# Keys and queries by token loads and DMA transposes, two output banks and a reordered start in a windowed-attention and softplus-MLP kernel

## The chip, the cores and the metric

One core of one Trainium2 chip. The metric is device microseconds of one execution of the whole kernel; the figure compared is the median of repeated runs. The engines are TensorE (PE; its weight loads are PEld), VectorE (DVE), ScalarE (ACT), GpSimd (POOL) and SyncE (SP), which here only issues DMAs.

## What is computed

Eight batches of eight heads, 576 positions, 64 elements per head. A query sees the keys within 32 positions; eight positions (global_idx) see all and are seen by all. The result of attention, 4,608 tokens by 512, goes through two matrix products with a softplus between.

```
scores = scale * np.matmul(q, k.transpose(0, 1, 3, 2))
mask = np.abs(pos[:, None] - pos[None, :]) <= 32
mask = mask | is_global[:, None] | is_global[None, :]
attn = softmax(where(mask, scores, -1e9))
x = np.matmul(attn, v)            # then (B, S, H*D) as 4608 x 512
h = x @ w_in                      # 512 -> 2048
g = np.maximum(h, 0.0) + np.log1p(np.exp(-np.abs(h)))
out = g @ w_out                   # 2048 -> 512
```

## The kernel before

**Attention of a batch.** A batch is four pairs of heads (p). Keys and queries are needed with the head's elements on the partitions (KT, QT: 128 partitions = two heads of 64, five blocks of 120 or 96 positions, each block followed by eight columns for the global positions). `load_runs` (L100) brings a batch of k to SBUF in one DMA on SP (float32, six positions to a partition, pieces of 1536 bytes) and a batch of q in one DMA on POOL's queue that casts to bfloat16. `cast_runs` (L137) reorders them on POOL into kqb, two heads at a time. `transposes` (L287) turns one pair: six PE transposes of 96 columns into one PSUM bank (tp, one bank in the main part) and, through `spread_columns` (L322), two DVE copies into KT or QT (L325, L327) and one or two small POOL copies (L330 to L333) that put in the global columns. For batches 3 to 7 these come from glob_T, which `global_columns` (L466) makes with PE from rows that `gather_rows` (L130) fetched, sixteen DMAs on POOL's queue. For batch 2 they come from `columns_of_2` (L458).

`products` (L343) multiplies keys and queries, `exponentials` (L358) is ACT's Exp, `mask` (L372) is DVE's product. `over_keys` (L385) forms both the sums (values all one) and the weighted values, in PSUM (av). `inv_ln` and `inv_exp` (L413, L421) make the reciprocal on ACT as exp(-ln), `scale_x` (L430) multiplies on DVE into xT. `glob_norm` (L446, DVE) and `glob_out` (L452, eight POOL copies, L455) put the rows of the global positions into xT. The values of a batch come in five DMAs of up to 120 tokens (`load_v`, L109, pieces of 256 bytes, on SP), are cast by POOL (`cast_v`, L143), and batch 2's are loaded by six casting DMAs on POOL's queue (`load_v_cast`, L118).

**The two products.** Nine tiles of 512 tokens. `mm1(n, kf)` (L478) makes one of 16 blocks of 128 columns of h: four matmuls into a bank h (two of them), then Exp and Ln with bias 1 on ACT, 512 columns each, into gts[n]. `mm2(n, s)` (L491) does a quarter of the products of 128 rows of the output: four matmuls into the one bank o; after the fourth quarter DVE copies to ot (two buffers) and SP stores.

**What sets the order.** The instruction order on every engine is written by hand. Ahead of the tile loop stand batch 0 and the begin of batch 1. Then (L683):

```
    for n in range(n_tiles + 1):
        for s in range(16):
            if n < n_tiles:
                mm1(n, s)
            attend(16 * n + s, 0)
            if n:
                mm2(n - 1, s)
            attend(16 * n + s, 1)
```

`attend` issues what the plan holds for that slot (16n+s) and half. `at(slot, half, f, ...)` fills the plan (L517), in the order of the calls. STARTS (L522) gives for each pair, in half slots, where its attention begins: batch 2 at slot 16, batch 3 at 28, batch 4 at 41, then every 16 slots. Loads stand some 20 slots ahead, casts some 12. An engine goes through its own instructions in this order and waits for semaphores only, so POOL and SP may run ahead of PE or hold it up. The first_rz buffer (L337, one of the two gt buffers) holds batch 0's reciprocals.

Of the kernel before, what the change touches and what calls it, by code (L numbers as in the profile page):

```python
# [11 lines left out]
FP32 = mybir.dt.float32  # L12
BF16 = mybir.dt.bfloat16
I32 = mybir.dt.int32
ALU = mybir.AluOpType
ACTF = mybir.ActivationFunctionType
# [3 lines left out]
P = 128  # L20
WIN = 32
KW = 120
NG = 8

ST = [120, 120, 120, 120, 96]
NTL = 5
WLO = [max(0, 128 * t - 40) for t in range(NTL)]
WHI = [128 * t + 160 for t in range(4)] + [512 + 96 + NG]
NPOS = WHI[-1]
SPLIT = 288  # L30
RUN = 6
NQ = 96
# [3 lines left out]
GOFF = {0: 0, 1: 160, 4: 360, 2: 0, 3: 200}  # L36
# [4 lines left out]
def kernel(  # L41
# [10 lines left out]
    nc = tc.nc  # L52
    B, H, S, D = q.shape
    NP = H // 2
    HD = H * D
    d_model, d_ff = moe_w_in.shape
    n_tokens = out.shape[0]
    KD, KF, NT = d_model // P, d_ff // P, 512
# [20 lines left out]
    KT = const.tile([P, NP, NTL, P], BF16)  # L79
    QT = const.tile([P, NP, NTL, P], BF16)  # L80
    V1 = [const.tile([P, NTL, HD], BF16, name=f"V1_{i}") for i in range(2)]
    runs = const.tile([NQ, H, RUN * D], FP32, name="k_f")
    v_f = const.tile([P, NTL, HD], FP32)
    GB = B - 3
    glob_2 = {n: const.tile([P, NP, NG], BF16, name=f"{n}_g2") for n in "kq"}
# [23 lines left out]
    def load_v(b, heads=slice(0, H)):  # L109
        for t in range(NTL):  # L110
            nc.sync.dma_start(out=v_f[:ST[t], t].rearrange("p (h d) -> p h d", d=D)[:, heads],
                              in_=v[b, heads, KW * t:KW * t + ST[t], :].rearrange("h s d -> s h d"))

    def load_v_rows(b):
        nc.sync.dma_start(out=v_f[KW:P], in_=v_rows[:, (b - 1) * HD:b * HD].unsqueeze(1).to_broadcast([NG, NTL, HD]))
# [171 lines left out]
    def transposes(n, b, p, copy=nc.vector.tensor_copy, unread=0):  # L287

        parts = [(slice(0, P), lambda r: kqb[n, b][:, r, p * P:(p + 1) * P])]
        if n == "q" and b < 2:  # L290
            parts = [(slice(64 * e, 64 * e + 64), lambda r, e=e: raw[b][:, 2 * p + e, r * D:(r + 1) * D]) for e in range(2)]
        if b == 1 and p:
            if n == "k":
                both[p] = region("tp")
            ps = both[p][:, 0:512] if n == "k" else both.pop(p)[:, 512:1024]
        else:
            ps = bank()[:]
        tb = ps.bitcast(BF16)
        for _ in range(unread):
            nc.tensor.matmul(out=ps, lhsT=junk[:, 0:P], rhs=junk[:], start=True, stop=True)  # L300
        for r in range(RUN):
            for o, of in parts:
                nc.tensor.transpose(out=tb[o, r * NQ:(r + 1) * NQ], in_=of(r), identity=ident_bf[:NQ, :NQ])  # L303
        if b < 2:
            g = ps[:, 384:384 + NG]
            for r in range(RUN):
                for o, of in parts:
                    nc.tensor.matmul(out=g[o], lhsT=of(r), rhs=onehot[:NQ, r, :],
                                     start=(r == 0), stop=(r == RUN - 1), skip_group_check=True)
        else:  # L310
            copy = nc.vector.tensor_copy
            g = glob_2[n][:, p] if b == 2 else glob_T[n][:, p].rearrange("p (g b) -> p b g", b=GB)[:, b - B + GB]
        spread = lambda: spread_columns(n, b, p, tb, g, copy)
        if b == 1 and p:
            both.setdefault((p, "copies"), []).append(spread)
            if n == "q":
                for f in both.pop((p, "copies")):
                    f()
        else:
            spread()  # L320
# [22 lines left out]
    def products(b, p, grp):  # L343
        sc = SC[p, grp] = region("sc")[:].rearrange("p (e c) -> p e c", e=2)
        biased = (b, p) in BIASED
        if biased:
            for e in range(2):
                nc.tensor.matmul(out=sc[:, e, 0:GW[grp]], lhsT=ident_bf[:], rhs=biases[grp], start=True, stop=False,
                                 skip_group_check=True)
        for i, t in enumerate(GRP[grp]):  # L350
            w = WHI[t] - WLO[t]
            for e in range(2):
                r = slice(64 * e, 64 * e + 64)
                nc.tensor.matmul(out=sc[:, e, GOFF[t]:GOFF[t] + w], lhsT=KT[r, p, t, :],  # L354
                                 rhs=QT[r, p].rearrange("p t c -> p (t c)")[:, WLO[t]:WHI[t]],
                                 start=not biased, stop=(not biased or i == len(GRP[grp]) - 1), skip_group_check=biased)

    def exponentials(b, p, grp):  # L358
# [119 lines left out]
    def mm1(n, kf):  # L478
        if kf == 0:
            gts[n] = work.tile([P, KF, NT], BF16, tag="gt", bufs=2, name="gt")  # L480
        hp = psum["pool"].tile([P, NT], FP32, tag="h", bufs=2)
        for kd in range(KD):
            nc.tensor.matmul(out=hp[:], lhsT=w_in_t[:, kd, kf * P:(kf + 1) * P], rhs=xT[:, kd, n * NT:(n + 1) * NT],  # L483
                             start=(kd == 0), stop=(kd == KD - 1))
        e = work.tile([P, NT], FP32, tag="e", bufs=2)
        nc.scalar.activation(out=e[:], in_=hp[:], func=ACTF.Exp)  # L486
        nc.scalar.activation(out=gts[n][:, kf, :], in_=e[:], func=ACTF.Ln, bias=1.0)  # L487

    ops = {}

    def mm2(n, s):  # L491
        i, part = s // 4, s % 4
        if part == 0:
            ops[n] = psum["pool"].tile([P, d_model], FP32, tag="o", name="o")
        op = ops[n]
        for kf in range(4 * part, 4 * part + 4):
            nc.tensor.matmul(out=op[:], lhsT=gts[n][:, kf, i * P:(i + 1) * P], rhs=w_out_t[:, kf, :],  # L497
                             start=(kf == 0), stop=(kf == KF - 1))
        if part == 3:
            ot = work.tile([P, d_model], FP32, tag="ot", bufs=2)  # L500
            nc.vector.tensor_copy(ot[:], op[:])  # L501
            nc.sync.dma_start(out=out[n * NT + i * P:n * NT + (i + 1) * P, :], in_=ot[:])

    CW = 512

# [11 lines left out]
    def at(g, half, f, *a):  # L517
        plan.setdefault((g, half), []).append((f, a))
# [11 lines left out]
    for p in range(NP):  # L530
        for n in "kq":
            at(8 + p // 2, 0, cast_runs, n, 2, pair_heads(p), nc.gpsimd.tensor_copy)
    at(9, 0, load_v_cast, 2)
    for i, n in enumerate("kq"):
        at(14 + i, 0, columns_of_2, n)
        at(27, i, global_columns, n)
        for g in range(NG):
            at(18 + g, 0, gather_rows, n, g)
    LOADS, CASTS = {3: (18, 20, 19)}, {3: (23, 26)}
    for b in range(1, B):  # L540
        g0 = 16 * (b - 1)
        if b > 2:
            loads = LOADS.get(b, (g0 - 22, g0 - 20, g0 - 17))
            at(loads[0], 1, load_runs, "k", b, every)
            at(loads[1], 1, load_runs, "q", b, every)
            at(loads[2], 1, load_v, b)
            at(loads[2], 1, load_v_rows, b)
            casts = CASTS.get(b, (g0 - 12, g0 - 9))
            for p in range(NP):
                for i, n in enumerate("kq"):  # L550
                    at(casts[0] + (4 * i + p) // 3, 0, cast_runs, n, b, pair_heads(p), nc.gpsimd.tensor_copy)
            for t in range(NTL):
                at(casts[1] + t // 3, 0, cast_v, b, t, nc.gpsimd)
        steps = {}

        def step(h, f, *a):
            steps.setdefault(h, []).append((f, a))

        for p in range(NP):
            if b == 1:  # L560

                to_transposes, to_scores, to_sums = (2 if p == 1 else 4 * p + 2), 4 * p + 4, 4 * p + 6
                to_inverse = to_x = to_sums
            else:
                h, pair = STARTS[4 * b - 8 + p], STARTS[4 * b - 7 + p] - STARTS[4 * b - 8 + p]
                to_transposes, to_scores, to_sums = h, h + pair // 2 + (pair == 7), h + pair
                to_inverse, to_x = to_sums + 1, to_sums + 2
            if (b, p) != (1, 0):
                step(to_transposes, transposes, "k", b, p)
                step(to_transposes + (b > 1), transposes, "q", b, p)  # L570
                for grp in range(2):
                    step(to_scores, scores, b, p, grp)
                for grp in range(2):
                    if (b, p) not in BIASED:
                        step(to_scores, mask, p, grp)
            step(to_sums, sums, b, p)
            step(to_sums, values, b, p)
            step(to_sums, inv_ln, b, p)
            step(to_inverse, glob_sums, b, p, 0)
            step(to_inverse, inv_exp, p)  # L580
            step(to_x, scale_x, b, p)
        step(to_x + (b > 1), glob_norm, b)
        step(to_x + (b > 1), glob_out, b)
        for h in sorted(steps):
            for f, a in sorted(steps[h], key=lambda fa: fa[0] is not transposes):
                at(h // 2, h % 2, f, *a)
# [138 lines left out]
```

## Time and profile before

| what | value |
|---|---|
| median of 14 runs | 368.59 us (365.36 to 371.0) |
| profiled execution | 368.92 us |
| its span | 367.3 us, mean clock granted to PE 0.995 |
| PE busy | 346.3 us, 94% |
| ACT busy | 272.8 us, 74% |
| DVE busy | 169.0 us, 46% |
| POOL busy | 132.1 us, 36% |
| SP's issues of token loads of v | 40, median 0.936 us each, landing after 5.2 us (median) |

The page gives busy times, the span in 40 slices, the chain of work that ended last and the costliest groups. In a timeline a row is: start, duration, engine, line, operation, written tile <- read tiles, shape, count, and in brackets the idle time before it and what ended it. Matmuls are pipelined, so durations on PE overlap: what a group takes is read from start to start. The profiled execution lies 1.6 us over its span, and this is the sum's base; the median of the runs is 0.3 us lower.

### The profile page before, as it was taken

Reading aid. Unit: us, or ns where it says so; the run is one execution under the profiler, and the core shown is the slowest. Engines: PE = TensorE matmul, PEld = TensorE weight load, DVE = VectorE, ACT = ScalarE, POOL = GpSimd, SP = SyncE. Lnnn points to the kernel's source line nnn. Section 1 sums busy time; section 2 is a strip of 40 time slices with the busy share of each in tenths; the row PEclk is TensorE's granted clock in tenths of the full one; section 3 lists DMA queues with packets and bytes.
Section 4 is the critical chain, followed back from the end, with each engine's and each line's share of the span. In section 5 each row is a group of like instructions: output and inputs, shape, how many; then the busy total and the mean of one; then the engine's idle time right before and its main releaser. Section 6 shows DMA issues by size and latency. Waiting matters only on the chain.

```text
span 367.3 us, 7712 instructions
## 1 busy us (share of the span) xinstructions
PE 346.3 (94%) x2981; PEld 173.5 (47%) x2981; DVE 169.0 (46%) x476; ACT 272.8 (74%) x433; POOL 132.1 (36%) x301
## 2 busy tenths in 40 slices
PE   7898897999899999999999999999999999999984
PEld 3565453454455545554555455545554444444431
DVE  7863432275576555655555556555553001001011
ACT  3677997687788888888888888888888667776500
POOL 7953949795157206430733074302001000000000
PEclk9999999899999999999999999999999999999999
DMA  7999999996628065806590758100000100100111
GB/s 174 199 225 216 216 195 231 90 211 149 98 59 142 14 160 93 168 32 157 95 168 29 159 94 166 32 29 31 29 32 34 52 29 30 57 29 30 57 57 57
DMA packets 63108, 37.87 MB, mean 103 GB/s; under 512 B 41672, under 2 KB 58224, under 8 KB 63072
## 3 DMA queue, kind: packets, MB, share of 16 engines
q1 hardware_dynamic: 44768, 27.63, 31.7%
q0 software_dynamic: 18160, 9.75, 20.2%
q8 instruction: 23, 0.38, 0.4%
q14 instruction: 13, 0.11, 0.1%
q10 hardware_dynamic: 144, 0.01, 0.0%
HBM read 37.56 MB, written 9.55 MB: 128 GB/s over the span
## 4 chain that ended last, share of the span: by engine, by line
PE 72%; POOL 7%; DMA 7%; DVE 5%; ACT 4%; issue 3%; POOLq 0%; DVEq 0%; ACTq 0%
PE o L497 33%; PE hp L483 28%; PE av L396 5%; PE tp L303 3%; PE sc L354 3%; DMA k_f<-in_k_dram 3%; DMA v_f<-in_v_dram 2%; DMA q_raw<-in_q_dram 2%; DVE ot L501 2%; POOL V L122 1%; POOL V L145 1%; DVE KT L325 1%; ACT rz L418 1%; ACT ex L365 1%; POOL kb L140 1%
## 5 line engine op out<-in xcount | busy, mean ns | idle before, releaser
L483 PE MATMUL hp<-xT,w_in_t 128*128 128x512 bf16 x576 | 148.6, 381 | 3.2 <-POOL xT L455 2.7
L497 PE MATMUL o<-w_out_t,gt 128*128 128x512 bf16 x576 | 146.5, 380 | 4.5 <-DVE ot L501 4.5
L486 ACT ACTIVATE e<-hp 128x512 f32<-128x512 f32 x144 | 85.9, 597 | 49.0 <-PE hp L483 46.9
L487 ACT ACTIVATE gt<-e 128x512 bf16<-128x512 f32 x144 | 90.7, 630 | 4.7
L497 PEld LDWEIGHTS <-gt 128*128 128x128 bf16 x576 | 54.5, 98 | 69.1 <-issue 9.9
L483 PEld LDWEIGHTS <-w_in_t 128*128 128x128 bf16 x576 | 52.3, 98 | 65.4 <-issue 7.7
L501 DVE COPY ot<-o 128x512 f32<-128x512 f32 x36 | 24.9, 691 | 73.2 <-PE o L497 71.5
L455 POOL COPY xT<-xg 128x4 bf16 x64 | 16.4, 256 | 95.9 <-DVE xg L450 92.5
L365 ACT ACTIVATE ex<-sc 128x1008 bf16<-128x1008 f32 (+1 forms) x56 | 48.5, 918 | 0.4 <-PE sc L354 0.4
L374 DVE TENSOR_TENSOR ex<-ex,mask 128x1008 bf16<-128x1008 bf16 (+1 forms) x48 | 34.1, 718 | 25.1 <-ACT ex L365 24.3
L325 DVE COPY KT<-tp 128x480 bf16<-128x480 bf16 x31 | 20.3, 655 | 35.4 <-PE tp L303 24.9
L145 POOL CAST V<-v_f 128x512 bf16<-128x512 f32 (+3 forms) x45 | 22.1, 531 | 27.5 <-DMA v_f<-v_global_rows 22.1
L140 POOL CAST kb<-k_f 96x768 bf16<-96x768 f32 x30 | 25.1, 856 | 4.2 <-DMA k_f<-in_k_dram 4.2
L406 DVE TENSOR_REDUCE gs<-av 128x8 f32<-128x32 f32 x64 | 12.0, 187 | 30.2 <-ACT rz L418 26.7
L418 ACT ACTIVATE rz<-av 128x616 f32<-128x616 f32 x28 | 19.0, 680 | 7.2 <-PE av L396 6.6
L325 DVE COPY QT<-tp 128x480 bf16<-128x480 bf16 x29 | 19.0, 657 | 10.5 <-PE tp L303 9.8
L434 DVE TENSOR_TENSOR xT<-av,rz 128x480 bf16<-128x480 f32 x28 | 18.4, 657 | 11.4 <-ACT rz L422 11.3
L140 POOL COPY qb<-q_raw 96x768 bf16<-96x768 bf16 x24 | 19.2, 825 | 10.7 <-DMA q_raw<-in_q_dram 8.8
L354 PE MATMUL sc<-QT,KT 64*128 64x200 bf16 (+2 forms) x320 | 20.2, 241 | 2.3 <-DVE xT L436 1.6
L422 ACT ACTIVATE rz<-rz 128x616 f32<-128x616 f32 x28 | 19.7, 703 | 0.2
L354 PEld LDWEIGHTS <-KT 64*128 64x128 bf16 x320 | 10.6, 94 | 18.6 <-issue 13.9
L396 PE MATMUL av<-ex,V 128*64 128x160 bf16 (+1 forms) x336 | 16.1, 229 | 1.3 <-POOL V L145 1.3
(126 smaller groups left out, 267.5 us busy)
## 6 DMA issues: line engine op xcount, KB each, us to landing
out_dram<-ot SPq DMA_DIRECT2D x36, 256.0 KB, 2.0
v_f<-in_v_dram SPq DMA_DIRECT2D x24, 240.0 KB, 5.7
k_f<-in_k_dram SPq DMA_DIRECT2D x5, 1152.0 KB, 10.7
k_f<-in_k_dram SPq DMA_DIRECT2D x12, 288.0 KB, 7.6
q_raw<-in_q_dram POOLq DMA_DIRECT2D x6, 576.0 KB, 6.0
w_in_t<-in_moe_w_in_dram POOLq DMA_DIRECT2D x4, 512.0 KB, 7.4
w_out_t<-in_moe_w_out_dram POOLq DMA_DIRECT2D x4, 512.0 KB, 13.9
v_f<-in_v_dram SPq DMA_DIRECT2D x6, 192.0 KB, 5.2
```

The lines of the kernel that those rows point to most:

```text
L140: copy(kqb[n, b][:, :, D * heads.start:D * heads.stop].rearrange("p r (h d) -> p h r d", d=D), (runs if n == "k" else raw[b])[:, heads].re ...
L145: eng.tensor_copy(V1[b % 2][:rows, t, cols], v_f[:rows, t, cols])
L325: copy(dst[:, p, 0:4, 0:KW].rearrange("p t (q r) -> p t q r", r=RUN), spread[:, 0:4 * NQT].rearrange("p (t q) r -> p t q r", q=NQT))
L354: nc.tensor.matmul(out=sc[:, e, GOFF[t]:GOFF[t] + w], lhsT=KT[r, p, t, :], rhs=QT[r, p].rearrange("p t c -> p (t c)")[:, WLO[t]:WHI[t]], s ...
L365: nc.scalar.activation(out=ex, in_=sc[:, :, 0:GW[grp]], func=ACTF.Exp, scale=SCALE)
L374: nc.vector.tensor_tensor(out=ex, in0=ex, in1=masks[grp][:, 0:GW[grp]].unsqueeze(1).to_broadcast([P, 2, GW[grp]]), op=ALU.mult)
L396: nc.tensor.matmul(out=av[64 * e:64 * e + 64, OFF + lo:OFF + hi], lhsT=weight(t, e), rhs=exps[p, grp][rows, e, c:c + hi - lo], start=(firs ...
L483: nc.tensor.matmul(out=hp[:], lhsT=w_in_t[:, kd, kf * P:(kf + 1) * P], rhs=xT[:, kd, n * NT:(n + 1) * NT], start=(kd == 0), stop=(kd == KD ...
L486: nc.scalar.activation(out=e[:], in_=hp[:], func=ACTF.Exp)
L487: nc.scalar.activation(out=gts[n][:, kf, :], in_=e[:], func=ACTF.Ln, bias=1.0)
L497: nc.tensor.matmul(out=op[:], lhsT=gts[n][:, kf, i * P:(i + 1) * P], rhs=w_out_t[:, kf, :], start=(kf == 0), stop=(kf == KF - 1))
L501: nc.vector.tensor_copy(ot[:], op[:])
```

## The change

1. *Output banks.* In tiles 1 to 7 the odd row groups write their products into the bank tp, the even ones stay in o. In the last tile all four use the two banks h. The last row group is made in two halves of 256 columns, each with 16 matmuls, a copy and a store.
2. *Tile 0's logarithm.* The exponentials of tile 0 go into first_rz (four areas of 512), and one Ln of 1024 columns serves two blocks.
3. *Batch 2's values* (`load_v_cast(2)`) move from slot 9 to slot 12.
4. *Tokens.* For batches 3 to 7, k, q and v come by token, five DMAs each on SP, spread over slots; k and q share one float32 buffer (kq_f, the former `runs`). POOL casts each to a bfloat16 tile with the tokens on the partitions, SP issues one DMA transpose for all pairs of a batch (128 x 2560 bfloat16, SBUF to SBUF) into KT/QT (even batches) or new tiles (odd ones), and POOL copies in the global columns of all pairs at once. The PE transposes of these batches and their DVE copies go. For batches 3 and 4 POOL first clears partitions 96 to 128 of the token tiles.

```
+    kq_f = const.tile([P, H * RUN * D], FP32, name="kq_f")
+    runs = kq_f[:NQ].rearrange("p (h c) -> p h c", h=H)
...
+    def tokens(n, b):
+        if (n, b) not in tok:
+            fresh = b < 5
+            tok[n, b] = work.tile([P, NP * NTL * P], BF16, tag=f"{n}b", bufs=2, name=f"{n}t") if fresh else tok[n, b - 2]
+            if fresh:
+                nc.gpsimd.memset(tok[n, b][96:P], 0.0)
+        return tok[n, b][:].rearrange("p (a t c) -> p a t c", a=NP, t=NTL)
+    def load_tokens(n, b, t):
+        o = kq_f if n != "v" else v_f[:].rearrange("p t c -> p (t c)")
+        nc.sync.dma_start(out=o[:ST[t], t * HD:(t + 1) * HD].rearrange("p (h d) -> p h d", d=D),
+                          in_=src[n][b, :, KW * t:KW * t + ST[t], :].rearrange("h s d -> s h d"))
+    def cast_tokens(n, b, t):
+        nc.gpsimd.tensor_copy(tokens(n, b)[:ST[t], :, t, :],
+                              kq_f[:ST[t], t * HD:(t + 1) * HD].rearrange("p (a c) -> p a c", a=NP))
+    def turn(n, b):
+        if b % 2:
+            turned[n, b] = work.tile([P, NP, NTL, P], BF16, tag="raw", bufs=2, name=f"{n}T")
+        else:
+            turned[n, b] = KT if n == "k" else QT
+        nc.sync.dma_start_transpose(out=turned[n, b][:].rearrange("p a t c -> p (a t) c"), in_=tok[n, b][:])
+    def spread_globals(n, b):
+        dst = turned[n, b]
+        g = glob_T[n][:].rearrange("p a (g b) -> p a b g", b=GB)[:, :, b - B + GB].unsqueeze(2)
+        if n == "k":
+            nc.gpsimd.tensor_copy(dst[:, :, :, KW:P], g.to_broadcast([P, NP, NTL, NG]))
+        else:
+            nc.gpsimd.tensor_copy(dst[:, :, 0:4, KW:P], g.to_broadcast([P, NP, 4, NG]))
+            nc.gpsimd.tensor_copy(dst[:, :, 4:5, ST[4]:ST[4] + NG], g)
...
+        if n == 0:
+            c = NT * (kf % 4)
+            e = first_rz[:].bitcast(FP32)
+            nc.scalar.activation(out=e[:, c:c + NT], in_=hp[:], func=ACTF.Exp)
+            if kf % 2:
+                nc.scalar.activation(out=gts[n][:, kf - 1:kf + 1, :].rearrange("p k c -> p (k c)"),
+                                     in_=e[:, c - NT:c + NT], func=ACTF.Ln, bias=1.0)
+            return
...
-            ops[n] = psum["pool"].tile([P, d_model], FP32, tag="o", name="o")
+            last = n == n_tiles - 1
+            ops[n] = psum["pool"].tile([P, d_model], FP32, tag="h" if last else "tp" if n and i % 2 else "o",
+                                       bufs=2 if last else 1, name="o")
...
+        if n == n_tiles - 1 and i == NT // P - 1:
+            if part % 2 == 0:
+                cols = slice(0, 256) if part == 0 else slice(256, 512)
+                if part:
+                    op = psum["pool"].tile([P, d_model], FP32, tag="h", bufs=2, name="o")
+                products_out(n, i, op[:, cols], range(KF), cols)
+                store(n, i, op[:, cols], cols)
+            return
...
-    at(9, 0, load_v_cast, 2)
+    at(12, 0, load_v_cast, 2)
...
+    def loads(b):
+        s0 = STARTS[4 * b - 8] // 2
+        if b == 3:
+            k0, kt, q0, qt, v0 = s0 - 12, s0 - 7, s0 - 8, s0 - 3, s0 - 5
+        elif b == 4:
+            k0, kt, q0, qt, v0 = s0 - 15, s0 - 10, s0 - 11, s0 - 6, s0 - 8
+        else:
+            k0, kt, q0, qt, v0 = s0 - 23, s0 - 15, s0 - 16, s0 - 8, s0 - 9
+        for n, first, last in (("k", k0, kt), ("q", q0, qt), ("v", v0, None)):
+            for t in range(NTL):
+                slot = first + (t // 2 if b < 5 else t)
+                at(slot, t % 2 if b < 5 else 1, load_tokens, n, b, t)
+                if n == "v":
+                    at(slot + 2, 1, cast_v, b, t, nc.gpsimd)
+                else:
+                    at(slot + 2, 0, cast_tokens, n, b, t)
+            if n == "v":
+                at(first, 0, load_v_rows, b)
+            else:
+                at(last, 0, turn, n, b)
+                at(max(last + 2, 28), 0, spread_globals, n, b)
...
-                step(to_transposes, transposes, "k", b, p)
-                step(to_transposes + (b > 1), transposes, "q", b, p)
+                if b < 3:
+                    step(to_transposes, transposes, "k", b, p)
+                    step(to_transposes + (b > 1), transposes, "q", b, p)
```

More of the change, by code (lines that the diff above doesn't have):

```diff
@@ L81 @@
     V1 = [const.tile([P, NTL, HD], BF16, name=f"V1_{i}") for i in range(2)]
-    runs = const.tile([NQ, H, RUN * D], FP32, name="k_f")
+    kq_f = const.tile([P, H * RUN * D], FP32, name="kq_f")
+    runs = kq_f[:NQ].rearrange("p (h c) -> p h c", h=H)
     v_f = const.tile([P, NTL, HD], FP32)
@@ L112, in load_v @@
                               in_=v[b, heads, KW * t:KW * t + ST[t], :].rearrange("h s d -> s h d"))
+    tok, turned = {}, {}
+    def tokens(n, b):
[26 more added lines that the diff above has]
+            nc.gpsimd.tensor_copy(dst[:, :, 4:5, ST[4]:ST[4] + NG], g)
     def load_v_rows(b):
@@ L311, in transposes @@
             copy = nc.vector.tensor_copy
-            g = glob_2[n][:, p] if b == 2 else glob_T[n][:, p].rearrange("p (g b) -> p b g", b=GB)[:, b - B + GB]
+            g = glob_2[n][:, p]
         spread = lambda: spread_columns(n, b, p, tb, g, copy)
@@ L349, in products @@
                                  skip_group_check=True)
+        kT, qT = turned.get(("k", b), KT), turned.get(("q", b), QT)
         for i, t in enumerate(GRP[grp]):
@@ L353, in products @@
                 r = slice(64 * e, 64 * e + 64)
-                nc.tensor.matmul(out=sc[:, e, GOFF[t]:GOFF[t] + w], lhsT=KT[r, p, t, :],
-                                 rhs=QT[r, p].rearrange("p t c -> p (t c)")[:, WLO[t]:WHI[t]],
+                nc.tensor.matmul(out=sc[:, e, GOFF[t]:GOFF[t] + w], lhsT=kT[r, p, t, :],
+                                 rhs=qT[r, p].rearrange("p t c -> p (t c)")[:, WLO[t]:WHI[t]],
                                  start=not biased, stop=(not biased or i == len(GRP[grp]) - 1), skip_group_check=biased)
@@ L489, with products_out, store @@
     ops = {}
+    def products_out(n, i, op, blocks, cols=slice(0, 512)):
+        for kf in blocks:
+            nc.tensor.matmul(out=op, lhsT=gts[n][:, kf, i * P:(i + 1) * P], rhs=w_out_t[:, kf, cols],
+                             start=(kf == 0), stop=(kf == KF - 1))
+    def store(n, i, op, cols=slice(0, 512)):
+        ot = work.tile([P, d_model], FP32, tag="ot", bufs=2)
+        nc.vector.tensor_copy(ot[:, cols], op)
+        nc.sync.dma_start(out=out[n * NT + i * P:n * NT + (i + 1) * P, cols], in_=ot[:, cols])
     def mm2(n, s):
@@ L493, in mm2 @@
         if part == 0:
-            ops[n] = psum["pool"].tile([P, d_model], FP32, tag="o", name="o")
+            last = n == n_tiles - 1
+            ops[n] = psum["pool"].tile([P, d_model], FP32, tag="h" if last else "tp" if n and i % 2 else "o",
+                                       bufs=2 if last else 1, name="o")
         op = ops[n]
-        for kf in range(4 * part, 4 * part + 4):
-            nc.tensor.matmul(out=op[:], lhsT=gts[n][:, kf, i * P:(i + 1) * P], rhs=w_out_t[:, kf, :],
-                             start=(kf == 0), stop=(kf == KF - 1))
+        if n == n_tiles - 1 and i == NT // P - 1:
[6 more added lines that the diff above has]
+            return
+        products_out(n, i, op[:], range(4 * part, 4 * part + 4))
         if part == 3:
-            ot = work.tile([P, d_model], FP32, tag="ot", bufs=2)
-            nc.vector.tensor_copy(ot[:], op[:])
-            nc.sync.dma_start(out=out[n * NT + i * P:n * NT + (i + 1) * P, :], in_=ot[:])
+            store(n, i, op[:])
     CW = 512
@@ L538 @@
             at(18 + g, 0, gather_rows, n, g)
-    LOADS, CASTS = {3: (18, 20, 19)}, {3: (23, 26)}
+    def loads(b):
[19 more added lines that the diff above has]
+                at(max(last + 2, 28), 0, spread_globals, n, b)
     for b in range(1, B):
@@ L542 @@
         if b > 2:
[L543 to L553, printed above, removed]
+            loads(b)
         steps = {}
```

## The prediction

> **What bounds the kernel now.** I read the page's shares first, then the busy time by stage, then each stage's PE timeline.
>
> ```profile
> PE 346.3 (94%) x2981; PEld 173.5 (47%) x2981; DVE 169.0 (46%) x476; ACT 272.8 (74%) x433; POOL 132.1 (36%) x301
> PE 72%; POOL 7%; DMA 7%; DVE 5%; ACT 4%; issue 3%; POOLq 0%; DVEq 0%; ACTq 0%
> ...
> 127.00:163.50 36.50, 36.07 (x312) 18.43 (x310) 21.25 (x55) 30.49 (x48) 15.07 (x34) 1.00 0.54 114
> ...
> 281.00:345.70 64.70, 64.18 (x295) 28.63 (x294) 7.42 (x13) 45.38 (x76) 1.62 (x8) 1.00 0.10 37
> 345.70:367.30 21.60, 14.59 (x65) 6.13 (x63) 3.46 (x5) 0.57 (x1) 0.00 (x0) 0.99 0.16 61
> ```
>
> The last three rows (columns: PE, PEld, DVE, ACT, POOL, granted clock, DMA share, GB/s) are one batch of the steady part, the tiles after attention and the tail. In the steady part PE is busy 36.07 of 36.5 us, and ACT, the next, 30.49. Time there is PE's stream. The tail is not: 14.59 of 21.6.
>
> The PE timeline of one pair of heads in the steady part (start, duration):
>
> ```profile
> 140.76 0.42 PE L303 MATMUL tp<-ident_bf,kb 96*128 96x96 bf16 x6
> 141.11 0.58 PE L396 MATMUL av<-ex,ones 128*64 128x160 bf16 x12
> ...
> 142.02 1.04 PE L483 MATMUL hp<-xT,w_in_t 128*128 128x512 bf16 x4
> 142.89 0.42 PE L303 MATMUL tp<-ident_bf,qb 96*128 96x96 bf16 x6
> 143.15 1.03 PE L497 MATMUL o<-w_out_t,gt 128*128 128x512 bf16 x4
> ```
>
> Start to start, the key transposes take 0.35 us and the query ones 0.26. The tail, and the one stall at the head of tile 1:
>
> ```profile
> 351.01 3.61 PE L497 MATMUL o<-w_out_t,gt 128*128 128x512 bf16 x16 [0.78 <-DVE ot L501]
> ...
> 354.67 0.69 DVE L501 COPY ot<-o 128x512 f32<-128x512 f32 x1 [3.70 <-PE o L497]
> ...
> 355.41 3.61 PE L497 MATMUL o<-w_out_t,gt 128*128 128x512 bf16 x16 [0.78 <-DVE ot L501]
> ...
> 57.04 4.45 POOL L122 DMA_DIRECT2D V<-in_v_dram  x5
> 61.49 2.06 POOL L455 COPY xT<-xg 128x4 bf16 x8
> ...
> 63.60 1.87 PE L483 MATMUL hp<-xT,w_in_t 128*128 128x512 bf16 x4 [2.04 <-POOL xT L455]
> ```
>
> Each tail group waits for the copy that frees the one bank o. At 63.60 PE waits for eight POOL copies that stood behind five DMA issues.
>
> **Part 1, banks and tail.** Groups start every 4.40 us (351.01, 355.41). Sixteen 512-column matmuls at the steady 0.216 (0.864 for four) take 3.46. With two banks the 0.94 between vanishes, also ahead of the first (346.62 instead of 345.69): 4 x 0.94 = 3.8 us. The last rows in halves are 32 matmuls of 256 columns, the same columns; a weight load with its transpose of 96 columns runs at 0.26/6 = 0.044 us, so 0.108 per matmul covers the loads. After the last matmul the copy has 256 columns: from the rows of 480 (0.656) and 96 (0.248) columns 0.42 instead of 0.69, 0.27 less. The store's latency stays. In the tiles before, one output group and its mm1 share take 6.98 us (290.73, 297.72) against 8 x 0.864 = 6.91: 0.07 per change of bank. With o and tp in turn that goes on some 17 changes (1.2 us), and so does the 0.52 at 283.75. What may eat it: tp is still written by the transposes of batch 2 and the global columns, but all of those fall beside tile 0's output, which keeps o. Sum 3.8 + 0.3 + 1.2 + 0.5 = 5.8; bounds 4.3 and 6.5.
>
> **Part 2, one logarithm for two blocks.** Tile 0's ACT has no gap over 0.3 us from 39.7 to 62.5: there ACT is the bound. An exponential and a logarithm cost 1.14 start to start. The slope of ACT from its rows of 1008 (1.009) and 800 columns (0.832) is 0.85 ns per column, so a logarithm of 1024 is 0.53 + 0.44 = 0.97 instead of 1.06; with one dependent step fewer 0.1 to 0.2 saved per pair, six pairs in the stretch: 0.9 us. The shared buffer (first_rz) holds batch 0's reciprocals, last read before the tile loop, so no wait from it.
>
> **Part 3, batch 2's values later.** POOL's six DMA issues (0.61 + 4.45) go behind the eight copies. The copies then start once the casts end and xg is there (57.0) and end at 59.1, before PE asks at 61.6. Gone are the 2.04 of wait and the slow matmuls after it (8 in 3.1 us instead of 1.73): 3.4. The price: the values land later. Issued from 57.04, they landed by 68 (7.3 to 10.3 us each). Now they start 2 us later and lie beside the new token loads of batch 3, which move k in 4,608 pieces of 256 B instead of 768 of 1536 B, while DMA is above 0.9 in that stretch. I put the landing at 71, between 70 and 74. PE asked for them at 73.7 and would now at 73.7 - 3.4 - 0.9 = 69.4. Behind that wait stand mm1, mm2 and all of ACT. So parts 2 and 3 give 2.7 together (bounds 0 and 4.3), the landing being the bound.
>
> **Part 4, tokens.** Removed from PE: per batch 48 transposes. Three pairs at 0.35 + 0.26, the first pair at 0.26 + 0.27 with a wait of 0.31 for DVE's KT copy (101.44): 1.83 + 0.84 = 2.67. Of the key's 0.35, some 0.09 is the change from mm2 to another shape, seen ahead of scores too (0.96 for 0.864), and stays: 2.4 a batch, five batches, 12.0 (to 13.3). DVE loses 16 copies, 7.2 us a batch, not on the path. ACT then has 30.5 of 34.1 us and a lag of some 0.6 us in its stretches; I take no new stall, up to 0.5 a batch.
>
> POOL: ten casts of 512 at 0.57 replace eight of 768 at 0.82, and three spreads replace twelve; lighter, except two memsets for each of batches 3 and 4 (32 partitions x 2560 bf16; from the 128x128 f32 memset at 0.234, 1.4 to 2.3 each).
>
> SP: the v token loads are the nearest row, 0.94 us an issue (0.4 to 1.1 undisturbed), 5.7 to landing. Fifteen a batch are 14.1; stores and global rows 2.5: 16.6 of 34 us, plus two transposes. A store behind them can be late by two groups (two ot buffers, two banks) before PE waits.
>
> The DMA transpose X itself (128 x 2560 bf16, 655 KB, SBUF to SBUF) is in no row. Lower end: the nearest transfer, a v load, moved 240 KB in some 1.5 us of a 7.6 us stretch (1.26 MB), so 655 KB take about 4 us. Against the change stands the Trainium skill, "VectorE: DVE Perf Modes", section "The three transpose paths": 390 ns for a 128x128 block on TensorE, 1309 ns by the DMA crossbar, and its rule is TensorE if PSUM will do. The row differs on the first: six transposes of 96 columns take 0.26 us here. By 1309 a transpose of 20 blocks would be 26 us; two of them and 16.6 on SP are 69 us in a 34 us period, a loss of 35 a batch. "DMA: Bandwidth & Descriptors", section "Latency and other measured facts", gives 261 GB/s for transposes: an estimate of 2.5 us, near 4.5 with a store's 2.0 of latency. The single-block figure is mostly latency, paid once; I take 4.5 (ends 4 and 26).
>
> With 4.5, batches 4 to 7 have 8 to 12 slots (16 to 25 us) from transpose to first use; hidden. Batch 3 has few. POOL's queue from 63.5: sixteen row gathers (9.1), casts 5.7, memsets 2.8 to 4.6, batch 2's spreads 2. Its query casts wait for loads that stand on SP behind the key transpose, which waits for POOL's key casts; the last gathers stand behind those casts. I get the last gather between 84 and 89, 4.3 to landing, so 88 to 93; PE asks for the global columns at about 90 (93.7 before). Stall 0 to 4; I take 2. The query transpose, spread at slot 28 and scores at slot 30 follow at 94 to 98 against PE's 99: met, with little to spare.
>
> Sum: 5.8 + 2.7 + 12.0 - 2 = 18.5. The profiled execution took 368.92 (span 367.3 and 1.6 around it), so 350.4; the median, 368.59, lies 0.3 lower: **350 us**.
>
> **Rivals.** *Batch 3's chain late*: SP and POOL wait for each other (casts, key transpose, query loads, casts, query transpose), 8 us more than I count, where X is some 8 us. For it: POOL is nearly gapless from 61.5 to 87, DMA above 0.9 until 82. Against: from batch 4 on there are many slots. PE stalls 8 to 10 at the global columns or the first scores: about 359.
> *The crossbar as bound, slower than before*: X exceeds (34 - 16.6)/2 = 8.7 us and SP falls behind every batch by 2X - 17.4. Five batches lose the 18.5 gained at X = 10.6; at 13, half the upper end, 5 x 8.6 = 43 more: about 393. For it: the 1309 ns figure. Against: that block is mostly latency.
> *The gain isn't there*: ACT and its two hp banks take over as PE's stream shortens, or PE clock is lost. Then only parts 1 to 3 count, about 360. Against: ACT would still have 3.6 us a batch free.
>
> **How the numbers follow.** Forecast 0.63; batch 3 late 0.18; crossbar as bound 0.11; ACT takes over 0.05; the rest (0.03) no change. The forecast's own range is 345 (all upper bounds, no stall) to 355; with the two middle rivals 345 to 362. Faster by over 0.5% (about what a measurement of this kernel tells from no change): 0.86, same 0.03, slower 0.11.
>
> **What would show it.** Tail groups every 3.46 us and no wait on ot; no xT wait at tile 1, with a V wait of up to 2 us instead; no tp groups after batch 2 and pairs every 8.5 us instead of 9.04 (141.11 to 150.15); SP rows of the transpose near 4.5 us; POOL's spreads waiting little except in batch 3. I am wrong if pairs stay at 9.04, if scores wait for turned keys or queries in batches 4 to 7, or if the stretch up to batch 3's first scores is longer than before.

## The result and the profile after

| what | before | after |
|---|---|---|
| median | 368.37 us (47 runs with those beside it; 368.59 in the 14 shown) | 351.1 us (350.36 to 355.28, 10 runs) |
| ratio | | 0.9563, 95% interval 0.953 to 0.9596 |
| profiled execution | 368.92 us, span 367.3 | 350.5 us, span 348.9 |
| PE | 94%, x2981 | 96%, x2757 |
| DMA packets | 63108 | 128169 |

One run each of experiments 1, 5 and 7, over 1.5% above the fastest of its kernel and at a lower granted clock, is left out of their figures.

The page's first and fourth part, then the busy time by stage, of the kernel after (columns: stretch, length, PE, PEld, DVE, ACT, POOL, granted clock, DMA share, GB/s):

```profile
PE 333.5 (96%) x2757; PEld 162.5 (47%) x2757; DVE 134.2 (38%) x397; ACT 270.0 (77%) x425; POOL 128.1 (37%) x265
...
PE 71%; DMA 10%; POOL 8%; issue 4%; ACT 3%; DVE 2%; POOLq 0%; SPq 0%; ACTq 0%
```

```profile
131.00:165.00 34.00, 34.00 (x264) 15.99 (x263) 14.06 (x38) 30.11 (x48) 15.01 (x29) 1.00 1.03 197
165.00:199.00 34.00, 34.00 (x264) 16.04 (x263) 14.06 (x38) 30.12 (x49) 12.16 (x26) 1.00 0.98 181
...
262.00:330.60 68.60, 68.60 (x339) 31.31 (x337) 9.29 (x19) 49.94 (x82) 1.62 (x8) 1.00 0.10 39
330.60:348.90 18.30, 14.96 (x86) 8.11 (x83) 3.62 (x6) 1.23 (x2) 0.00 (x0) 1.00 0.19 72
```

PE is the bound as before, now without a gap (34.00 of 34.00), and its stream is shorter. The last but one column has changed most: the 16 DMA engines were 0.54 busy in such a stretch and are now at 1.0. That share adds up the time of packets and has no end at 1 (it reads 1.20 from 61.4 to 99.9 us of this kernel). PE doesn't wait for it in this stretch; the experiments come back to it.

A pair of the steady part, and the tail, on PE:

```profile
136.12 0.58 PE L434 MATMUL av<-ex,ones 128*64 128x160 bf16 x12
...
140.59 0.64 PE L392 MATMUL sc<-QT,KT 64*128 64x160 bf16 x10
141.16 1.04 PE L521 MATMUL hp<-xT,w_in_t 128*128 128x512 bf16 x4
...
144.72 0.58 PE L434 MATMUL av<-ex,ones 128*64 128x160 bf16 x12
```

```profile
330.68 14.88 PE L540 MATMUL o<-w_out_t,gt 128*128 128x512 bf16 x84
```

A pair takes 8.60 us (136.12 to 144.72) instead of 9.04, and no tp group stands in it. The last 84 matmuls run in one piece. What PE waits for in the whole execution now (us in total, times, longest):

```profile
PE sc L392 <- DVE xT L474: 1.8, 3, 0.8
...
PE hp L521 <- POOL xT L493: 1.4, 2, 0.8
PE tp L509 <- DMA hot_v<-in_k_dram: 1.2, 1, 1.2
...
PE o L540 <- DVE ot L545: 0.7, 1, 0.7
```

The one new resource, the transpose on SP's queue, at its first two uses (start, duration of the issue):

```profile
74.38 4.36 SPq L140 DMA_TRANSPOSE kT<-kt  x1
...
88.02 4.48 SPq L140 DMA_TRANSPOSE qT<-qt  x1
```

Over all ten the issue takes 3.0 to 4.6 us and the data have landed after 5.0 (median; 4.9 to 6.4).

**Where the time went**, by five points that both traces have:

| up to | before | after | gained in the stretch | forecast |
|---|---|---|---|---|
| batch 2's first sums | 73.66 | 70.09 | 3.6 | 2.7 |
| batch 3's first scores | 103.53 | 99.87 | 0.1 | -1.2 |
| the last sums of batch 7 | 277.83 | 265.01 | 9.1 | 11.8 |
| tile 7's last output group | 344.81 | 330.68 | 1.3 | 1.1 |
| the end of the span | 367.3 | 348.9 | 4.3 | 4.1 |

The forecast column puts part 4's first pair (0.84) and the stall (-2) into the second row, 11.2 of part 4 and 0.6 of the bank changes into the third.

### The profile page after: what moved, and what is told of

Read it like the earlier page. It is cut to its first block, busy times and chain, and to the rows that moved or that the text cites. A ratio compares the mean times of both kernels' runs of the same rounds, so it can differ in the third digit from the quotient of the medians.

```text
span 348.9 us, 7185 instructions
## 1 busy us (share of the span) xinstructions
PE 333.5 (96%) x2757; PEld 162.5 (47%) x2757; DVE 134.2 (38%) x397; ACT 270.0 (77%) x425; POOL 128.1 (37%) x265
## 2 busy tenths in 40 slices
DMA packets 128169, 47.34 MB, mean 136 GB/s; under 512 B 114288, under 2 KB 123416, under 8 KB 128136
## 3 DMA queue, kind: packets, MB, share of 16 engines
q1 hardware_dynamic: 113752, 40.09, 56.9%
q0 software_dynamic: 14240, 6.80, 14.5%
## 4 chain that ended last, share of the span: by engine, by line
PE 71%; DMA 10%; POOL 8%; issue 4%; ACT 3%; DVE 2%; POOLq 0%; SPq 0%; ACTq 0%
PE o L540 32%; PE hp L521 30%; PE av L434 5%; PE sc L392 3%; DMA kq_f<-in_k_dram 3%; DMA v_f<-in_v_dram 2%; DMA q_raw<-in_q_dram 2%; DMA hot_v<-in_k_dram 2%; POOL kt L123 1%; POOL kt L132 1%; DMA kq_f<-in_q_dram 1%; ACT ex L403 1%; POOL V L159 1%; PE sc L385 1%; POOL q_raw L108 1%
## 5 line engine op out<-in xcount | busy, mean ns | idle before, releaser
L540 PE MATMUL o<-w_out_t,gt 128*128 128x512 bf16 (+1 forms) x592 | 145.3, 373 | 0.7 <-DVE ot L545 0.7
L533 ACT ACTIVATE e<-hp 128x512 f32<-128x512 f32 x128 | 76.2, 595 | 37.8 <-PE hp L521 36.4
L534 ACT ACTIVATE gt<-e 128x512 bf16<-128x512 f32 x128 | 80.6, 630 | 4.1
L545 DVE COPY ot<-o 128x512 f32<-128x512 f32 (+1 forms) x37 | 24.9, 672 | 66.5 <-PE o L540 66.5
L132 POOL CAST kt<-kq_f 120x512 bf16<-120x512 f32 (+1 forms) x25 | 15.8, 650 | 17.1 <-DMA kq_f<-in_k_dram 16.8
L132 POOL CAST qt<-kq_f 120x512 bf16<-120x512 f32 (+1 forms) x25 | 15.3, 621 | 15.0 <-DMA kq_f<-in_q_dram 14.8
L434 PEld LDWEIGHTS <-ones 128*64 128x64 bf16 x384 | 12.5, 109 | 11.3 <-issue 10.9
L434 PE MATMUL av<-ex,ones 128*64 128x160 bf16 (+1 forms) x336 | 16.7, 233 | 0.5 <-DVE ex L412 0.4
L392 PE MATMUL sc<-QT,KT 64*128 64x200 bf16 (+2 forms) x200 | 13.4, 242 | 1.9 <-DVE xT L474 1.0
L434 PEld LDWEIGHTS <-V 128*64 128x64 bf16 x384 | 13.5, 110 | 1.4 <-POOL V L182 0.8
```

Source lines behind the costliest of these rows:

```text
L132: nc.gpsimd.tensor_copy(tokens(n, b)[:ST[t], :, t, :], kq_f[:ST[t], t * HD:(t + 1) * HD].rearrange("p (a c) -> p a c", a=NP))
L392: nc.tensor.matmul(out=sc[:, e, GOFF[t]:GOFF[t] + w], lhsT=kT[r, p, t, :], rhs=qT[r, p].rearrange("p t c -> p (t c)")[:, WLO[t]:WHI[t]], s ...
L434: nc.tensor.matmul(out=av[64 * e:64 * e + 64, OFF + lo:OFF + hi], lhsT=weight(t, e), rhs=exps[p, grp][rows, e, c:c + hi - lo], start=(firs ...
L540: nc.tensor.matmul(out=op, lhsT=gts[n][:, kf, i * P:(i + 1) * P], rhs=w_out_t[:, kf, cols], start=(kf == 0), stop=(kf == KF - 1))
L545: nc.vector.tensor_copy(ot[:, cols], op)
```

## The experiments

The median of the kernel before was 368.1 to 368.4 us beside them.

**1. Start and end alone, and 2. tokens alone.** The first leaves keys and queries on PE. It can't have the second bank in tiles 1 to 7: the transposes of a pair need tp while an output group would hold it.

```
-            ops[n] = psum["pool"].tile([P, d_model], FP32, tag="o", name="o")
+            last = n == n_tiles - 1
+            ops[n] = psum["pool"].tile([P, d_model], FP32, tag="h" if last else "o", bufs=2 if last else 1, name="o")
```

> The changes to the start and the end alone; keys and queries of all batches still turned on PE. Since the transposes need the bank tp in tiles 1 to 7, only the last tile has two output banks here. Theory (each part is paid where the traces show it: 3.6 us up to batch 2's first sums, 4.3 in the tail): 368.4 - 7.9 = 360.5 us. Rival (the token loads took nothing off the path, the whole gain is start and end): 351. Pairs in the steady part stay at 9.04 us by both.

Measured 361.8 us (ratio 0.9833, 0.9754 to 0.9912): the theory's 360.5 lies within the interval, the rival's 351 does not. In its profile (span 363.1) the tail's 4.3 us are there (last sums to end 85.1 us instead of 89.5), and from batch 3's first scores to the last sums it takes 174.3 us, as before.

The start is hard to read from this profile. PE is 3 us late in it before the first changed instruction: the row `tp<-V,hot_v` begins at 22.57, against 19.38 before and 19.52 in the full change, since up to 16.6 us its matmuls took longer (three of 512 columns 1.46 us instead of 0.82, at a granted clock that reads 1.00; why, the trace doesn't show). From that row to batch 2's first sums it takes 50.0 us, against 54.3 before and 50.6 in the full change.

The second is the full change with the former output step, a logarithm per block and slot 9:

> The token loads and DMA transposes alone: one bank o, whole rows in the tail, a logarithm per block, batch 2's values at slot 9. Theory: the stretch from batch 3's first scores to the last sums shrinks by some 9 us as in the full change, start and tail are as before: 368.4 - 9 = 359.4 us. Rival (the token loads pay only because the start runs earlier, or give part of it back in batch 3): 362 or more.

Measured 358.3 us (0.9738, 0.9656 to 0.982), the theory's size. From batch 3's first scores (102.39) to the last sums (267.63) it takes 165.2 us, as the full change does (165.1), against 174.3 before. So the token loads alone carry 9 to 10 of the 17 us. This profile too has PE 3 us late (22.60); with the start's former order it takes 50.3 us from that row to the first sums. POOL is not late by as much, so a late PE finds the copies into xT sooner done, and neither of the two profiles shows what the start's change is worth. By the ratios the two parts save 1.7% and 2.6%, the full change 4.4%: within the intervals they add up, and what the bank that only the tokens set free is worth in tiles 1 to 7 is too small to be read from the difference.

**3. Batch 2's values at slot 9.**

```
-    at(12, 0, load_v_cast, 2)
+    at(9, 0, load_v_cast, 2)
```

> The full change with batch 2's values issued at slot 9 again, ahead of the eight copies into xT. Theory (the copies behind the issues are the stall): PE waits some 2 us at the head of tile 1 and runs slower for two groups after it, 351.1 + 3 = 354 us. Rival (the landing of the values or POOL's queue for batch 3 is what counts, so that earlier values give the time back): 351 to 352.

Measured 353.0 us (0.9628, 0.9555 to 0.970), not apart from the full change. But no execution took that time: two took 350.3 and 351.6 us at a granted clock of 1.00, as the rival says, and two took 354.4 and 354.9 at 0.995 and 0.989, as the theory says. The profile is of the fastest of the four. Head of tile 1, then the values:

```profile
62.04 1.02 PE L521 MATMUL hp<-xT,w_in_t 128*128 128x512 bf16 x4 [1.02 <-POOL xT L493]
...
71.83 0.25 PE L434 MATMUL av<-ex,V 128*64 128x144 bf16 x2 [0.18 <-DMA V<-in_v_dram]
```

The wait for the eight copies is 1.02, not 2.04, and no slow matmuls follow. The slow ones in the profile of before are a lower granted clock: 0.54 from 63.6 to 66.7 us, behind the wait, where it reads 1.00 here. POOL's casts of batch 2's queries ended at 54.9 here and at 56.4 there: the start depends on when a load lands and differs between executions, so part of the 3.4 us that I read off one of them was its luck. Whether the two slower executions had that stall, and whether slot 12 makes it rarer, stays open. The first sums come 0.6 us later than in the full change. And the values, issued four microseconds earlier, are waited for (0.18) where in the full change they were not: no landing bound from slot 12.

**4. One output bank in all tiles.**

> The full change with the former output step: one bank o in all tiles, whole rows at the end. Theory: four waits of 0.94 us and 0.27 of copy in the tail come back (4.1), 0.07 us at some 27 changes of bank before it (1.9): 351.1 + 6 = 357 us. Rival (only the tail counts, the small gaps hide under other waits): 355.

Measured 358.1 us (0.9726, 0.9659 to 0.9794), 7 over the full change. From the last sums (267.05) to the end it takes 89.6 us instead of 83.9, so 5.7 lie there; 2.5 more stand ahead of batch 3's scores, where this execution waited 2.9 us for the row gathers. Part 1 is shown, at about its forecast, by the 5.7.

**5. and 6. The transposes twice and three times,** batches 4 to 7, into dead tiles. The kernel with two takes only the first of the two destinations in the list:

```
         nc.sync.dma_start_transpose(out=turned[n, b][:].rearrange("p a t c -> p (a t) c"), in_=tok[n, b][:])
+        if b > 3:
+            for o in [tok[n, b - 1], tok['q' if n == 'k' else 'k', b - 1]]:
+                nc.sync.dma_start_transpose(out=o[:].rearrange("p (a c) -> p a c", c=P), in_=tok[n, b][:])
```

> Each DMA transpose of batches 4 to 7 issued a second time, into a token tile that is dead by then; the output's data is as before. SP's issues of the transposes take 3.0 to 4.6 us (3.8 on average), so SP has 14.1 + 2.5 + 4 x 3.8 = 31.8 us of work in a period of 34.4. Theory (the transposes lie off the path, with room for as much again): 351 to 352 us. Rival (the crossbar is close to the bound, or SP's queue is): 2 us or more per batch, 359 and up, with PE waiting for turned keys and queries or for the stores.

> The same with two more transposes each: SP has 16.6 + 6 x 3.8 = 39.4 us of work in a period of 34.4 and falls behind 5 us a batch over four batches. By the prediction's threshold (a transpose of over 8.7 us loses 2X - 17.4 per batch; here X = 11.4): 351 + 4 x 5.4 = 372 us. Rival (the lead of 8 to 12 slots, 16 to 25 us, swallows it, since only four batches fall behind): 351 to 356.

Measured 360.7 us (0.9793, 0.9729 to 0.9856) and 389.8 (1.0582, 1.0518 to 1.0647). My theory fell: ten and thirty-nine us, where 0 and 21 at most were expected; with two the size is the rival's. PE's long waits with three:

```profile
PE av L437 <- DVE ex L415: 13.1, 5, 5.2
PE sc L395 <- POOL QT L151: 8.7, 1, 8.7
PE av L437 <- POOL V L185: 7.4, 6, 2.1
```

Part of the loss is slower matmuls: PE's busy time is 333.5 us after the change, 337.5 with two and 344.0 with three, at a granted clock of 1.00, 0.989 and 0.956. The rest, 6 and 30 us, is waiting.

What the added transposes cost the DMA engines is in the queue's share of 16 engines' span, after, twice, three times (one from each page):

```profile
q1 hardware_dynamic: 113752, 40.09, 56.9%
```

```profile
q1 hardware_dynamic: 134488, 45.33, 64.0%
```

```profile
q1 hardware_dynamic: 155224, 50.57, 65.9%
```

Times the spans (348.9, 359.1, 388.9) these are 198.5, 229.8 and 256.3 us: eight more transposes take the 16 engines 31.3 and 26.5 us more, some 3.6 each, in 2,592 packets; two more a batch are 7.2 us. Neither the share nor what the engines move has risen above the full change's 1.03 and 197 GB/s by much. A stretch with two, and one with three (columns as above):

```profile
165.00:200.00 35.00, 31.93 (x239) 14.88 (x238) 12.06 (x35) 26.34 (x43) 10.71 (x24) 0.95 1.10 193
```

```profile
131.00:275.00 144.00, 118.87 (x833) 54.86 (x831) 43.83 (x122) 98.08 (x155) 35.03 (x80) 0.89 1.01 192
```

The path in the trace runs through the order of SP's queue. With two:

```profile
142.59 3.05 SPq L140 DMA_TRANSPOSE kT<-kt  x1
145.70 3.19 SPq L143 DMA_TRANSPOSE kt<-kt  x1
148.93 0.58 SPq L128 DMA_DIRECT2D kq_f<-in_q_dram  x1
...
152.62 0.61 POOL L132 CAST qt<-kq_f 120x512 bf16<-120x512 f32 x1 [4.48 <-DMA kq_f<-in_q_dram]
```

The query load stands behind the added transpose, and POOL's cast waits 4.48 us for it, where it waits 1.75 in the full change; the next transposes wait for those casts. From batch 4 to batch 7 the key transposes follow each other every 30.3 us in the full change, 36.9 with two and 44.4 with three, while a batch takes PE 34.4 us in the full change. So this round of SP and POOL still runs ahead of PE in the full change, and each further pair of transposes lengthens it by some 7 us. That is the added issues on SP (6.3) as much as the added time of the engines (7.2): these two runs don't separate them. SP was busy some 0.83 of the stretch in both (0.64 in the full change), so my count of its busy time alone would not have shown the loss.

**7. The same DMA time without SP.** One load beside each transpose, on POOL's queue:

```
+        if b > 3:
+            nc.gpsimd.dma_start(out=tok[n, b - 1][:NQ].rearrange("p (h c) -> p h c", h=H),
+                                in_=src[n][b].rearrange("h (p r) d -> p h (r d)", r=RUN)[:, :, 0:320])
```

> The full change with one more load beside each DMA transpose of batches 4 to 7: 96 x 8 pieces of 1280 bytes, cast to bfloat16, issued on POOL's queue into a token tile that is dead by then; the output's data is as before. By the traces such a load takes the 16 DMA engines some 3.6 us (4.3 for the former query load of 1536-byte pieces), about what a second transpose took (3.9), but SP issues nothing more. Theory (after the change the 16 DMA engines are the full resource, 1.0 busy in batches 3 to 6, with a lead of some 18 us): as with transposes issued twice, 359 to 361 us. Rival (SP's queue was what overflowed there): 351 to 352.

Measured 365.2 us (0.9900, 0.9839 to 0.9961). POOL's queue took 22.4% of 364.2 us instead of 14.5% of 348.9, 31.0 us more for eight loads, as much as the second transposes. SP issued nothing more, but the 113,752 packets of its queue took 59.4% of 364.2, 216.3 us instead of 198.5, and its transposes of batches 4 to 7 landed after 8.3 to 8.8 us instead of 4.9 to 5.4: the time of a packet is not fixed, it grows beside other transfers. From batch 3's first scores to the last sums the profile takes 11.0 us more than the full change (9.1 with transposes twice); 4 more lie ahead of the first extra load. PE waits behind POOL:

```profile
148.80 1.02 PE L524 MATMUL hp<-xT,w_in_t 128*128 128x512 bf16 x4 [3.05 <-POOL xT L496]
...
188.03 1.86 PE L524 MATMUL hp<-xT,w_in_t 128*128 128x512 bf16 x4 [2.52 <-POOL xT L496]
```

and POOL waits for turned keys and queries (36 us in all, 12.5 in the full change). So it takes no further instruction on SP to lose the time: more transfers on the DMA engines are enough, and SP's own issues take longer with them (a transpose 3.3 to 6.5 us). That the extra load also sits in POOL's queue (0.77 us each, 6 us in all) can't explain the 11.

**8. The clears on DVE.** `nc.gpsimd.memset` of the token tiles becomes `nc.vector.memset`.

> The four clears of 32 x 2560 on DVE instead of POOL, 2.23 us each there. Theory (batch 3's chain of POOL and SP is late by little: the global columns wait 1.2 us for the last gathers, tile 2's first product 0.76 for the copies into xT): both waits go, 351.1 - 1.5 to 2 = 349.4 us. Rival (what ends those waits is DMA, saturated in that stretch, and not POOL's work): 351.

Measured 353.6 us (0.9605, 0.9569 to 0.9642), 2.5 more. The theory fell. POOL's first key cast waits for DVE (the releaser named is PE's av; the clear itself is DVE's at 70.93):

```profile
72.18 1.16 POOL L132 CAST kt<-kq_f 120x512 bf16<-120x512 f32 x2 [6.01 <-PE av L434]
```

On POOL, which runs ahead of PE, the clear cost 2.23 us at 65.9. On DVE it takes 1.12 (shown as 32x1280 uint32), but DVE's order puts it behind batch 2's mask products, at 70.9, and the cast waits 6.0 us for it. PE then waits 2.6 us for the gathers, not 1.2.

**9. The reciprocal's second step earlier** (batches 3 to 7):

```
-                to_inverse, to_x = to_sums + 1, to_sums + 2
+                to_inverse, to_x = (to_sums, to_sums + 1) if b >= 3 else (to_sums + 1, to_sums + 2)
```

> For batches 3 to 7 the second ACT step of the reciprocal is issued straight after the first, half a slot earlier, and the product with it likewise. Theory (since the transposes are gone, the second half of each pair's scores waits some 0.08 us for scale_x, which frees its PSUM region): pairs of 8.51 instead of 8.59 us, 19 x 0.08 = 1.5 us less, 349.6. Rival (the 0.08 is PE's own change of shape, or ACT's Exp for mm1 comes later in exchange): 351 or more.

Measured 350.6 us (0.9516, 0.9482 to 0.955): the fastest median of all, 0.5 below the change, and not apart from it by the intervals. The mechanism is shown by the pairs, 8.52 us (250.17 to 258.69), and by the scores, which take 0.56 again:

```profile
250.17 0.58 PE L434 MATMUL av<-ex,ones 128*64 128x160 bf16 x12
...
254.64 0.56 PE L392 MATMUL sc<-qT,kT 64*128 64x160 bf16 x10
258.69 0.52 PE L434 MATMUL av<-ex,ones 128*64 128x160 bf16 x10
```

So the 0.08 in the full change's pair is a wait, too short to be listed: scale_x's last piece there ends at 166.60, with the scores begun at 166.37. From batch 3's first scores to the last sums this profile takes 163.1 us instead of 165.1. The medians show 0.5 of it; this execution lost the rest and more ahead of batch 3, where it waited 3.1 us for the gathers.

**10. Gathers earlier, and 11. with the reciprocal too.**

```
-            at(18 + g, 0, gather_rows, n, g)
+            at(16 + g, 0, gather_rows, n, g)
+    at(9, 0, tokens, "q", 3)
```

> The full change with the sixteen row gathers two slots earlier and the clear of batch 3's query tile moved to slot 9, into POOL's idle 2.3 us before the copies into xT. Theory (the last gathers stand on POOL behind query casts that wait for loads behind the key transpose on SP): the wait of 1.2 to 3.1 us for the gathers at the global columns goes, 349 to 350 us. Rival (the gathers land late because DMA is full, whenever they are issued): 351.

> The same with the second step of the reciprocal issued straight after the first (batches 3 to 7), which took the pairs from 8.59 to 8.52 us. Theory (the two act in different stretches, so they add): 348.5 us. Rival (one takes the place of the other): 350.

Measured 356.3 us (0.9680, 0.9636 to 0.9725) and 354.0 (0.9608, 0.957 to 0.9645). The wait for the gathers did go, and a dearer one came, of the first of them:

```profile
PE sc L392 <- POOL QT L369: 5.8, 3, 2.2
```

Batch 2's small copies of the global columns now stand on POOL behind gathers and casts: the query copy ran at 69.92, where PE asked for it at 68.8. I had looked at who waits for the gathers and not at what stands behind them. The reciprocal's move adds (2.3 us here).

**12. Two logarithms.** The branch for tile 0 is taken out.

> The full change with a logarithm for each block of tile 0 again. Theory (ACT bounds tile 0; 0.1 to 0.2 us a pair over six pairs): 351.1 + 0.9 = 352 us. Rival (tile 0's end waits for the copies into xT or batch 2's columns anyway): 351.

Measured 351.2 us (0.9553, 0.951 to 0.9596) against 351.1. The interval would admit the theory's 0.9; the profiles don't show it, and the rival held. Tile 1's first product starts at 61.47 there and at 61.44 in the full change: the long logarithm stands ahead of an exponential that frees hp, and PE waits 0.79 us for it:

```profile
55.93 1.89 PE L521 MATMUL hp<-xT,w_in_t 128*128 128x512 bf16 x8 [0.79 <-ACT first_rz L527]
```

## Why the prediction was right, and where it was not

The time (350 forecast, 351.1 measured) and the main cause are right: PE's stream was the bound in the steady part, it lost the transposes, and the larger part of the gain lies where the sum put it (the tail, and the stretch from batch 3 to batch 7). That the sum comes so close is in part luck: part 4 gave some 2.7 us less than forecast, and the start gained 3.6 in the profiles that is not shown to be the change's. None of the signs of being wrong appeared. The steps:

- **Part 1**, 5.8 forecast: 4.3 in the tail, 1.3 in the tiles before, and experiment 4 takes back 5.7 after the last sums. Right.
- **Part 2**, 0.9: nothing to be seen (experiment 12). ACT's sum is shorter, but the step from ACT to PE is not: the exponential that PE waits for comes later.
- **Part 3**, "the landing being the bound": wrong. The values were not waited for; first sums came at 70.09. What slot 12 gives is 0.6 us in profiles side by side, not distinguished from nothing in the runs; the 3.4 of stall and slow matmuls (granted clock 0.54) came from one execution in which the queries landed late. That the stretch as a whole gained 3.6 may be mostly that difference between executions: in experiment 3's profile the former slot reaches the first sums at 70.69, not at 73.66. The profiles here don't resolve it.
- **Part 4**, 12.0: some 9 to 10. The transposes went as forecast; the missing term is a wait that I had set at nothing (at most 0.5 a batch): without the transposes PE reaches the scores before scale_x has freed their region (0.08 us a pair, 0.76 once at batch 3; experiment 9), and 0.76 stands at tile 2 for the copies into xT. Together these are 3.0 us, about what is missing.
- **The transpose**, 4.5 chosen between 4 and 26: 5.0 to landing. The 1309 ns per block of the Trainium skill ("VectorE: DVE Perf Modes", section "The three transpose paths") would be 26.2; twenty blocks in one transfer are 0.25 each. The row of the nearest load was the right base. No run here turns a single block, so why one alone costs more is not shown.
- **Batch 3's chain**, a stall of 2: 1.2 at the global columns, as described (query casts behind loads behind the key transpose). The gathers' last issue was at 87.2, within the 84 to 89. Right in kind; 1.2 to 3.1 us by execution.
- **The rival "crossbar as bound"** had the wrong threshold. I counted SP's busy time (16.6 us and two issues) as if the queue could be filled up. I left out that SP and POOL wait for each other in every batch, and the DMA engines' own time, though the stretch of before showed a share of 0.54: a batch of v in pieces of 256 bytes took them some 8 us there, k and q some 5.8 and 4.3 in long pieces. With k and q at v's price and two transposes of 3.6 the sum is 31 us of a batch's 34, before the stores. A transpose of 8.7 us would not have been free: with each issued twice (3.0 to 5.4 us an issue on SP, 3.6 of the engines) the kernel already loses 10 us. The forecast held because with one transpose the loads still run ahead of PE.
- **ACT takes over**: did not happen, ACT 30.1 of 34.0.

## What to carry to other kernels

When work moves from a bound engine to DMA, sum the time of the 16 DMA engines for a period, and follow one round of loads, casts and transposes through the queues in order; the busy time of the issuing queue is not enough. Here the share went from 0.54 to 1.0 without a loss, and two more transposes or loads a batch, in four batches, then cost 10 to 14 us. After PE's stream is shortened, ask which producer it now reaches too early; a wait of 0.08 us is in no list and adds up to 1.5 us in nineteen pairs. Before a stall is counted as gain, see in a second execution whether it is there. A step moved forward on a queue that runs in order (gathers, clears) moves all behind it: name those first.

## What the runs showed of the hardware

- One DMA transpose of 128 x 2560 bfloat16 within SBUF: issue 3.0 to 4.6 us on SP, landing 5.0 (8.3 to 8.8 beside further loads, experiment 7), some 3.6 us of the 16 engines, 2,592 packets.
- The same clear (32 x 2560 bfloat16) takes POOL 2.23 us and DVE 1.12, where the row shows it as 32 x 1280 uint32.
- The start is not the same from execution to execution: batch 2's first sums came between 70.1 and 71.4 us in seven kernels with an identical start of the program up to there, and in two others PE was 3 us late at 22.6 us, ahead of any change. Differences of a microsecond in one profile's start prove nothing.
- The granted clock fell behind some waits of PE: to 0.54 from 63.6 to 66.7 us behind the 2.04 in the profile of before, and to 0.89 on average from 131 to 275 us of experiment 6, where PE waited up to 8.7 us.
